# Loading each streamed slice of the query weights in two transfers, of 120 and of 8 rows

## Chip, core and metric

The kernel runs on one core of a Trainium2 chip. The metric is the device time of one launch in microseconds, as the median of several runs. Engines are named as in the profile: PE is TensorE's matmul stream and PEld its weight loads, DVE is VectorE, ACT is ScalarE, POOL is GpSimd, SP is SyncE, whose queue issues nearly all transfers from HBM.

## What is computed

Two layers are applied in turn, A, B, A, B, each to the layer norm of its input and added to it. The sequence has 2048 tokens of 640 values.

```python
# A: attention with a memory that is carried from segment to segment
mem = mem0                                   # 8 rows
for s in range(64):                          # segments of 32 tokens
    h = concat([mem, x[32*s : 32*s+32]])     # 40 rows
    q, k, v = h @ Wq, h @ Wk, h @ Wv         # 640 -> 32 heads x 192
    p = softmax(mask(q @ k.T * 192**-0.5))
    o = (p @ v) @ Wo                         # back to 640
    mem, out[s] = o[:8], o[8:]
# B: token mixing and a two-layer MLP
h   = gelu(layernorm(x) @ w1)
x1  = x + shifted_quarters(h) @ w2
out = x1 + gelu(layernorm(x1) @ w3) @ w4     # 640 -> 1536 -> 640
```

The memory makes A a recurrence: segment s+1 needs the output of segment s. All weights are bf16[...].

## The kernel before

The two A layers run as two lanes of one pipeline. Step t works on segment t of the first A layer and on segment t-5 of the second, so that each weight tile is used for 2 x 40 = 80 columns. There are 69 steps (`T_A = NSEG + LAG`). Between them `chunk` and `chunk_end` do layer B for 64 tokens of each lane, once in two steps.

In a step, `attention_step` goes through four pairs of head groups (`NPAIR`), each group of four heads. For a pair, `proj_pair` makes keys, queries and values, in this order. The weights of one pair and kind are a matrix of 640 x 1536, held as five slices of 128 rows (`KC = 5`, `PW = 1536`). Some slices stay on chip for the whole run; the others are streamed again in every step:

```python
STREAM = {"k": 3, "q": 3, "v": 2}
RING_A = 7
```

So a step streams four times three key, three query and two value slices, 8 x 4 = 32 transfers of 128 rows x 3072 bytes. `load_pair` adds one SP operation for each (line 431), into one of seven ring slots called `wst`. Each slice is used by 12 matmuls with their weight loads (line 507). `load_b` streams layer B's weights through three slots called `wstB` (lines 454 to 460). Resident slices (`wk`, `wq`, `wv`, and `wo`) are loaded once, at line 415.

The order of all work is made ahead of time: every operation is added to a `Plan` with an engine, an estimated duration and a due time, and `place` lays them out in time, each engine taking the earliest possible operation with the earliest due time. SP's operations have an estimated duration of `DMA_ISSUE` (0.37 us in the plan). The planned transfer service (`srv`) limits how early a transfer may be placed; one that is placed at that limit is called `paced`. When the program is written out in the planned order, each paced transfer is made to wait for the last PE operation planned to be done by then:

```python
        elif o.paced:
            k = len(done) - 1
            while k >= 0 and done[k].end + PE_LAT > o.start:
                k -= 1
            if k >= 0:
                tc.add_manual_dep(o.last, done[k].last.name, dep, reason="pace")
```

Apart from this, a transfer waits until its slot was read by PE, and until the transfer that used its landing semaphore before has landed. SP's transfers use eight such semaphores in turn. A matmul group's first weight load waits for the slice's semaphore.

## Time and profile before

| | |
|---|---|
| median of three runs | 3676.43 us (3671.96 to 3677.07) |
| the profiled execution's own time | 3664.71 us |
| its span, first to last instruction | 3663.0 us |
| mean granted TensorE clock | 0.982 |
| mean transfer rate over the span | 302 GB/s |
| issues of streamed query, key and value slices | 828, 828 and 552 |
| issues of layer B's weights | 525 of 320 KB and 140 of 160 KB |

The profile is of one execution. A row of the waits names the waiting engine and line, then what released it, the total in us, how often, and the longest. A row of the transfer queues gives packets, megabytes, and the time of the packets as a share of 16 transfer engines over the span. A row of issues shows SP's instruction, with the least, median and greatest time that SP spent on it. Apart from these views the prediction uses single records of the trace: the start and length of each transfer packet, and the times at which semaphores were raised.

### The profile page before, as it was taken

To read this page: it belongs to the slowest core of one execution; us is meant where nothing else is said; L and a number is where in the kernel's file an instruction comes from. 1 tells how busy PE (TensorE), PEld (TensorE's weight loads), DVE (VectorE), ACT (ScalarE), POOL (GpSimd) and SP (SyncE) were. 2 spreads that over 40 slices of the span, in tenths; PEclk is the share of its full clock that TensorE was granted. 3 is DMA by queue.
4 is the path that set the end of the run, shared out by engine and by line. 5 is a ranking of instruction groups with operands and counts; after the bars stand their busy time and mean duration, and the time that the engine had idled before them with its cause. 6 is when DMAs were issued, how large, how long until landed. Compare 5 with 4: busy or idle time off the path is not lost. (4 is left out here: it accounts for less than half of the span.)

```text
span 3663.0 us, 188705 instructions
## 1 busy us (share of the span) xinstructions
PE 3438.2 (94%) x84703; PEld 3279.3 (90%) x84703; DVE 2583.9 (71%) x7716; ACT 1530.9 (42%) x3586; POOL 247.8 (7%) x467
## 2 busy tenths in 40 slices
PE   5889999999999999999999999999999999999984
PEld 4788999999999999999999999999999999998873
DVE  2456777777777777777777777777777777776653
ACT  1233444444444444444444444444444444443331
POOL 0000000000000000000000000000000000000000
PEclk9999999999999999999999999999999999999996
DMA  9898988889888988889888898888988998889993
GB/s 318 296 313 293 319 301 304 303 311 322 307 301 302 313 311 304 304 306 322 305 309 306 299 322 302 309 306 300 322 295 309 309 313 309 297 296 304 317 304 111
DMA packets 512602, 1107.61 MB, mean 302 GB/s; under 512 B 50862, under 2 KB 223036, under 8 KB 511792
## 3 DMA queue, kind: packets, MB, share of 16 engines
q1 hardware_dynamic: 504560, 1082.42, 86.2%
q8 instruction: 662, 10.85, 1.2%
q0 software_dynamic: 7232, 13.13, 1.1%
q14 instruction: 148, 1.21, 0.1%
HBM read 1090.10 MB, written 5.24 MB: 299 GB/s over the span
## 5 line engine op out<-in xcount | busy, mean ns | idle before, releaser
L507 PEld LDWEIGHTS <-wst 128*128 128x128 bf16 x26496 | 1091.8, 100 | 108.3 <-DMA wst<-in_A_Wq_dram 42.8
L632 PE MATMUL psy<-oT,wo 128*128 128x80 bf16 (+1 forms) x16560 | 666.8, 199 | 35.6 <-issue 17.9
L632 PEld LDWEIGHTS <-wo 128*128 128x128 bf16 x16560 | 614.8, 100 | 42.8 <-issue 24.0
L517 ACT CAST qT<-psq 128x480 bf16<-128x480 f32 (+1 forms) x552 | 286.2, 529 | 791.8 <-PE psq L507 790.8
L507 PE MATMUL psq<-hT,wst 128*128 128x80 bf16 (+1 forms) x9936 | 494.5, 199 | 33.9 <-DMA wst<-in_A_Wq_dram 30.4
L507 PE MATMUL psk<-hT,wst 128*128 128x80 bf16 (+1 forms) x9936 | 477.5, 199 | 17.7 <-DMA wst<-in_A_Wk_dram 15.5
L621 DVE CAST oT<-pso 128x480 bf16<-128x480 f32 (+1 forms) x552 | 339.3, 619 | 193.7 <-PE pso L615 190.6
L507 PE MATMUL psv<-hT,wv 128*128 128x80 bf16 (+1 forms) x9936 | 432.9, 199 | 2.6 <-issue 2.6
L579 DVE CUSTOM_DVE_ANT_1 pss<-pss,mask 80x320 f32<-80x320 f32 (+1 forms) x512 | 244.9, 478 | 208.7 <-PE pss L568 165.4
L507 PEld LDWEIGHTS <-wv 128*128 128x128 bf16 x9936 | 383.5, 100 | 9.2 <-issue 3.1
L553 ACT COPY V<-pvt 80x384 bf16<-80x384 bf16 (+1 forms) x552 | 261.8, 474 | 270.0 <-PE pvt L544 249.6
L507 PE MATMUL psv<-hT,wst 128*128 128x80 bf16 (+1 forms) x6624 | 354.4, 199 | 13.7 <-DMA wst<-in_A_Wv_dram 6.8
L605 ACT COPY PT<-pst 80x320 bf16<-80x320 bf16 (+1 forms) x552 | 221.9, 402 | 320.6 <-PE pst L600 248.9
L531 DVE CAST kT<-psk 64x160 bf16<-64x160 f32 (+1 forms) x1104 | 336.6, 305 | 8.9
L537 ACT CAST vF<-psv 128x480 bf16<-128x480 f32 (+1 forms) x552 | 290.4, 526 | 122.4 <-PE psv L507 119.5
L507 PE MATMUL psk<-hT,wk 128*128 128x80 bf16 (+1 forms) x6624 | 319.0, 199 | 15.9 <-ACT hT L650 11.3
L507 PE MATMUL psq<-hT,wq 128*128 128x80 bf16 (+1 forms) x6624 | 318.9, 199 | 5.3 <-DMA wq<-in_A_Wq_dram 3.1
L525 DVE CAST kT<-psk 128x320 bf16<-128x320 f32 (+1 forms) x552 | 255.5, 463 | 96.9 <-PE psk L507 89.3
L586 ACT ACTIVATE Pm<-pss,sm 80x320 bf16<-80x320 f32 (+1 forms) x552 | 275.5, 504 | 101.4 <-DVE sm L579 100.8
L590 DVE TENSOR_REDUCE sm<-Pm 80x4 f32<-80x320 bf16 (+1 forms) x552 | 250.2, 453 | 75.9 <-ACT Pm L586 67.6
L544 PE MATMUL pvt<-ident,vF 128*80 128x128 bf16 (+1 forms) x3312 | 285.4, 223 | 8.2 <-ACT vF L537 5.3
L551 DVE COPY V<-pvt 80x384 bf16<-80x384 bf16 (+1 forms) x552 | 190.6, 349 | 139.0 <-ACT V L553 118.8
(108 smaller groups left out, 4561.5 us busy)
## 6 DMA issues: line engine op xcount, KB each, us to landing
wst<-in_A_Wk_dram SPq DMA_DIRECT2D x828, 384.0 KB, 5.0
wst<-in_A_Wq_dram SPq DMA_DIRECT2D x828, 384.0 KB, 5.0
wst<-in_A_Wv_dram SPq DMA_DIRECT2D x552, 384.0 KB, 5.0
wstB<-in_B_w_dram SPq DMA_DIRECT2D x525, 320.0 KB, 4.8
wstB<-in_B_w_dram SPq DMA_DIRECT2D x140, 160.0 KB, 4.6
wo<-in_A_Wo_dram SPq DMA_DIRECT2D x8, 960.0 KB, 7.4
wv<-in_A_Wv_dram SPq DMA_DIRECT2D x4, 1152.0 KB, 7.0
wk<-in_A_Wk_dram SPq DMA_DIRECT2D x4, 768.0 KB, 6.1
```

Of the source, the lines that this page charges most:

```text
L507: nc.tensor.matmul(out=o[:, cc, 0:N], lhsT=wv(kc, GW * j + cc * P, GW * j + (cc + 1) * P), rhs=h[:, kc, c0:c0 + N], start=(kc == 0 and cc ...
L517: nc.scalar.copy(out=q[:, :, 0:N], in_=T(pq)[:, :, 0:N])
L525: nc.vector.tensor_copy(out=k4[:, :, 0::3, 0:N], in_=p4[:, :, 0::2, 0:N])
L531: nc.vector.tensor_copy(out=k4[r0:r1, :, jj, 0:N], in_=p4[r0:r1, :, 1, 0:N])
L537: nc.scalar.copy(out=vf[:, :, 0:N], in_=T(pq)[:, :, 0:N])
L544: nc.tensor.transpose(out=o[0:N, c * P:(c + 1) * P], in_=vf[:, c, 0:N], identity=ident[:, :])
L553: nc.scalar.copy(out=dst, in_=src)
L579: nc.vector.tensor_tensor_reduce(out=o, in0=o, in1=maskt.unsqueeze(1).to_broadcast([N, HG, N]), scale=-scale, scalar=3.0e38, op0=ALU.add, ...
L586: nc.scalar.activation(out=Pb[0:N, :, 0:N], in_=o, func=ACT.Exp, bias=sm_[0:N, 0:1], scale=-1.0)
L590: nc.vector.tensor_reduce(out=sm_[0:N, 2:2 + HG], in_=Pb[0:N, :, 0:N], axis=AX.X, op=ALU.add)
L621: nc.vector.tensor_copy(out=o_[:, :, 0:N], in_=T(pso)[:, :, 0:N])
L632: nc.tensor.matmul(out=o[:, m, c0:c0 + N], lhsT=wo[:, cc, m * P:(m + 1) * P], rhs=o_[:, cc, 0:N], start=st, stop=True, skip_group_check=True)
```

## The change

Each streamed slice of the query weights is loaded by two transfers into the same slot: rows 0 to 119, then rows 120 to 127. Streamed key and value slices stay as they were, with one transfer. The plan counts two issues for such an operation, and the wait for pace goes to the first of its two transfers.

```diff
             def fn(op, b=b, kc=kc):
-                nc.sync.dma_start(out=T(b)[:, 0:PW], in_=w_src[kind][:, kc, cols])
-            add("SP", DMA_ISSUE, due - now + 0.01 * j, fn, w=(b,), dma=2 * P * PW, queue="wa")
+                if kind == "q":
+                    nc.sync.dma_start(out=T(b)[0:120, 0:PW], in_=w_src[kind][0:120, kc, cols])
+                    nc.sync.dma_start(out=T(b)[120:P, 0:PW], in_=w_src[kind][120:P, kc, cols])
+                else:
+                    nc.sync.dma_start(out=T(b)[:, 0:PW], in_=w_src[kind][:, kc, cols])
+            add("SP", DMA_ISSUE * (2 if kind == "q" else 1), due - now + 0.01 * j, fn, w=(b,), dma=2 * P * PW, queue="wa")
             slots.append(b)
...
         o.last = nc.cur_bb.bb.instructions[-1]
+        first = nc.cur_bb.bb.instructions[-2] if o.e == "SP" and o.d > DMA_ISSUE else o.last
...
-                tc.add_manual_dep(o.last, done[k].last.name, dep, reason="pace")
+                tc.add_manual_dep(first, done[k].last.name, dep, reason="pace")
```

## Prediction

> **What bounds the kernel now.** I read the page first, then the busy time by stretch, then the waits of TensorE, then SP's queue, and last the single records of transfers and semaphores.

> ```profile
> span 3663.0 us, 188705 instructions
> PE 3438.2 (94%) x84703; PEld 3279.3 (90%) x84703; DVE 2583.9 (71%) x7716; ACT 1530.9 (42%) x3586; POOL 247.8 (7%) x467
> ...
> q1 hardware_dynamic: 504560, 1082.42, 86.2%
> q8 instruction: 662, 10.85, 1.2%
> ```

> TensorE is busy 94% of the span, and the transfer engines spend 86.2% of it on SP's queue q1. VectorE and ScalarE have room. The stretch table says that the middle is fuller than the average:

> ```profile
> 500.00:1000.00 500.00, 489.76 (x12036) 473.34 (x12034) 376.33 (x1089) 224.34 (x511) 34.48 (x63) 1.00 0.90 309
> ```

> The columns after the length are PE, PEld, DVE, ACT, POOL, then the clock, the transfer engines' share and GB/s. PE is busy 489.8 of 500 us at full clock, transfers 0.90. So the bound is TensorE, with a weight stream close behind it, and a change of the stream can act only on the idle remainder. What that remainder waits for:

> ```profile
> PEld L507 <- DMA wst<-in_A_Wq_dram: 42.8, 80, 3.7
> PEld L507 <- issue: 35.5, 74, 1.7
> ...
> PEld L507 <- DMA wst<-in_A_Wk_dram: 23.7, 47, 2.4
> ...
> PEld L507 <- DMA wst<-in_A_Wv_dram: 11.4, 28, 0.7
> ```

> Columns: total us, times, longest. Streamed weights stop the weight loads for 42.8 + 23.7 + 11.4 = 78 us, the query weights most. "Issue" is a wait that nothing in the profile explains. PE has 60 gaps of over 0.25 us without a releaser, 46 us in all; I set them beside the packets of q8, the instruction stream, and 57 of them end 1.0 to 2.0 us after the end of such a 16 KB packet. There TensorE waits for its own instructions.

> The issue side:

> ```profile
> L431 SPq DMA_DIRECT2D wst<-in_A_Wq_dram x828: 327/328/1695, 9.9 to 3569.2; - x166
> ...
> DMA to landing us min/median/max: 3.2/5.0/7.4
> ```

> An issue takes SP 0.328 us (median), a load lands 5.0 us after it. The smallest step from issue to issue is 0.379 us; after a query load it is never below 0.706. SP is paced by PE (its largest wait is for psk), so it has time.

> **One engine ends the loads.** In the semaphore records a load posts 16 completions. Between first and last lie 1.83 us (median), and the last is 0.54 us behind the fifteenth. This last one is one and the same engine: its distance to the eighth is 1.12 us half a microsecond after the start of an instruction packet and 1.70 us two microseconds after it, while the fifteenth stays at 0.74 to 0.84. An instruction packet takes 1.04 us; 662 of them on one engine are 689 us, 18.8% of the span, on top of its 86.2%. These sums count overlapping packets, but this engine has no reserve. Which number it has, the trace does not say.

> [...]the load of h2u at the start posts one early update and then 8, where a 128-row load posts 16. No 120-row transfer is shown.[...]

> **The change, part by part.** The order of instructions on PE, VectorE, ScalarE and GpSimd stays as it was, and SP's order too, with each of the 828 query loads doubled.

> 1. *SP.* 828 more issues at 0.328 us are 272 us of SP time, one beside each query load; the eight-row load of h2u took 0.36 us, so I price both halves alike. A pair takes 0.379 + 0.328 = 0.71 us, and the next issue came after 0.706 us at the least: nothing is pushed. The pace's wait moves to the first half, so the second does not stand behind it. Were a 120-row issue to cost 0.6 us, some gaps would be overrun by up to 0.3 us; that is inside the ladder below. Upside: none.
> 2. *Landing semaphores.* SP's transfers take eight in turn, and an issue waits until the transfer eight places earlier has landed. Now that margin is 2.4 us or more in 99 of 100 cases. With pairs, eight places hold fewer loads: putting the old times into the new sequence, 133 of 3101 issues come too early, by 50 us together, 90 of them value loads. Queued behind a held value load are the next key loads and TensorE's first value group; their slack (next item) hides most of it. My count gives 1 to 3 us.
> 3. *Rows.* A 3072-byte packet takes 121 ns (median) and a semaphore packet 9. [...]+130 ns a load, +828 x 0.130 = 108 us each, 2.9% of the span. Three query loads come close together, so the delay adds up to 0.39 us where the engine has no pause; laid on the issue times, it is 0.19 us in the mean.[...]
> 4. *Ports.* [...]Completions of a load are spread over some 1.3 us without the last, so a random pair is 0.43 us apart; my estimate is 0.25 us a load, with bounds 0 and 0.94.
> 5. *TensorE's second wait.* The first weight load of each query tile waits for two semaphores, the second in an instruction of its own. TensorE's sequencer has 247 such now, 51 ns each, and the matmuls after them start 36 ns after the one before, as everywhere: hidden[...]. Where PE really waits (about 160 times) it may show: 0 to 8 us; I take 2.

> **What lateness costs.** For each query load I took the time from landing to first use. Of 828, 133 have under 0.1 us, 195 under 0.3, 259 under 0.5, 391 under 1.0. Making all of them late by d, summing what exceeds the slack, and crediting each stall to the loads already in flight gives:

> | d, us | 0.13 | 0.26 | 0.45 | 0.6 | 1.0 |
> |---|---|---|---|---|---|
> | added, us | 11 | 25 | 50 | 74 | 145 |

> **Forecast (0.53): slower.** The last completion of a query load is on a nine-row engine and later than the last one now, either because the slow engine is among them[...]. d = 0.19 + 0.25 = 0.44 us, about 49 us by the ladder; + 2 for held issues, + 2 for the second wait = 53. Against the profiled execution's own 3664.7 us this is 3718. That execution is 0.3% below the median of the runs, 3676.4; on their scale I give 3726, rounding the sum to 50. The case's own range is +11 (rows alone) to +145, so 3687 to 3821. Against it: the slow engine may be the one that is spared.

> **Rival 1 (0.33): faster, because engine 15 is the slow one.** Then query loads end on the next engine: -0.54 + 0.19 = -0.35 us, and key and value loads profit too. Of the waits for streamed weights, 0.36 us each would give back 24 (query) + 13 (key) + 9 (value) = 46 us; each stall removed takes slack from the loads in flight, so I count 60%, 28 us. Instructions come in sooner as well: a quarter of 46 us, 12. Together -40: 3636, between -10 and -80. It decides at a port loss of about 0.35 us a load: above that, nothing of it is left.[...]

> **Rival 2 (0.14): within 0.2%**, 3676. The slow engine is one of 8 to 14, or relief and ports cancel. A microsecond or two of held issues is all. For it: what is not last costs nothing.

> **Rival 3 (within the 0.53, 0.05 of it): the 120 rows are dealt differently[...]**, over eight engines. Then these take 15 + 1 rows, 0.97 us more a load, 803 us each, 22% on top of 86.2%: they exceed the span, and the end is at 1.08 x 3663, over 3950.

> **Numbers.** A difference of 0.2%, 7 us, is about what can be told from none. Faster 0.33, same 0.14, slower 0.53. The likeliest case gives 3726; the range goes from 3622, most of rival 1, to 3805, which leaves out the upper end of the port bound and rival 3: about 0.1 on each side.

> **What the profile after would show.** Rows: q1's packets up by some 828 x 7 = 5,800, with the same bytes. Forecast right: the waits for in_A_Wq grow from 42.8 to about 90 us, and those for key and value stay or grow. Rival 1: waits for Wq, Wk, Wv and "issue" all shrink. Item 1 wrong: the median issue of a query half is well above 0.33 us. Item 2 wrong: SP's waits name transfers for over 100 us, and value waits grow. The forecast falls if the waits for Wq do not grow; its mechanism falls if the end is later while Wq's waits stay.

## The result, and the profile after

The changed kernel takes 4079.7 us (median of four runs, 4076.0 to 4088.0) against 3674.7 us before (median of four): 1.111 times as long, 95% interval 1.109 to 1.113, or +405 us. I had forecast slower, with 3726 us and a range up to 3805. The direction was right and the size was wrong by a factor of eight.

The page of the changed kernel, the lines that answer to those of before:

```profile
span 4086.3 us, 190432 instructions
PE 3539.9 (87%) x84703; PEld 3343.0 (82%) x84703; DVE 2584.9 (63%) x7716; ACT 1533.1 (38%) x3586; POOL 248.0 (6%) x467
...
q1 hardware_dynamic: 510356, 1082.45, 88.5%
q0 software_dynamic: 7232, 13.13, 1.2%
q8 instruction: 666, 10.91, 1.2%
```

TensorE fell from 94% to 87%, while the transfer engines' share on q1 rose, from 86.2% to 88.5%, of a span that is 423 us longer. The bytes are the same. So SP's packets took 0.885 x 4086 = 3616 us of each engine's time where they had taken 0.862 x 3663 = 3157: 459 us more, somewhat more than the 405 us lost. 5,796 packets came in, 828 x 7 as foreseen, and those are far too few to explain it: the packets themselves became slower. The mean 3072-byte packet in the records went from 140 to 162 ns, and 31% of them lie between 160 and 260 ns, where before 92% had taken less than 130.

The loss is not all waiting. Of the 423 us, 102 are busy time of PE, for the same 84,703 matmuls. The mean granted clock fell from 0.982 to 0.966; by an estimate, 3438 x (0.982 / 0.966 - 1), that accounts for 57 of them. The other 321 us are idle time. Kernels of this case that lost more show a lower clock, by and large (0.981 at +121 us, 0.976 at +302, 0.967 at +391); that the stalls lowered it is not shown.

The stretch from 500 to 1000 us (PE, PEld, DVE, ACT, POOL, clock, transfers' share, GB/s):

```profile
500.00:1000.00 500.00, 443.32 (x10514) 424.46 (x10512) 328.03 (x951) 196.06 (x445) 32.06 (x58) 0.98 0.90 269
```

The same 0.90 of busy transfer engines now moves 269 GB/s, not 309.

The waits of the weight loads:

```profile
PEld L511 <- DMA wst<-in_A_Wq_dram: 293.0, 313, 2.3
PEld L511 <- issue: 73.1, 136, 2.4
PEld L511 <- DMA wst<-in_A_Wk_dram: 63.0, 92, 2.4
```

All waits for streamed weights went from 78 to 359 us, +281, of which +250 at query slices and +39 at key slices, with -9 at value slices. The waits called "issue" at this line doubled. SP's own issues stayed cheap:

```profile
L432 SPq DMA_DIRECT2D wst<-in_A_Wq_dram x828: 324/325/1683, 9.9 to 3991.9; - x166
L433 SPq DMA_DIRECT2D wst<-in_A_Wq_dram x828: 271/297/1647, 10.3 to 3992.4; - x166
```

The profile has no time to landing for this kernel, because the eight-row half posts other numbers of completions. Read from the semaphore records, the 120-row half lands 6.35 us after its issue (median; 5.02 before for 128 rows), the eight-row half 5.49, and the value slices that follow 5.96 instead of 4.94. The key slices land as soon after their issue as before (5.0 us), although their waits grew: these loads were issued late for TensorE.

### The profile page after: what moved, and what is told of

Read it like the earlier page. It is cut to its first block, busy times and chain, and to the rows that moved or that the text cites. A ratio compares the mean times of both kernels' runs of the same rounds, so it can differ in the third digit from the quotient of the medians.

```text
span 4086.3 us, 190432 instructions
## 1 busy us (share of the span) xinstructions
PE 3539.9 (87%) x84703; PEld 3343.0 (82%) x84703; DVE 2584.9 (63%) x7716; ACT 1533.1 (38%) x3586; POOL 248.0 (6%) x467
## 3 DMA queue, kind: packets, MB, share of 16 engines
q1 hardware_dynamic: 510356, 1082.45, 88.5%
## 5 line engine op out<-in xcount | busy, mean ns | idle before, releaser
L511 PEld LDWEIGHTS <-wst 128*128 128x128 bf16 x26496 | 1114.1, 100 | 417.8 <-DMA wst<-in_A_Wq_dram 293.0
L511 PE MATMUL psq<-hT,wst 128*128 128x80 bf16 (+1 forms) x9936 | 532.1, 201 | 277.5 <-DMA wst<-in_A_Wq_dram 268.4
L636 PE MATMUL psy<-oT,wo 128*128 128x80 bf16 (+1 forms) x16560 | 676.5, 200 | 64.3 <-issue 41.2
L511 PEld LDWEIGHTS <-wq 128*128 128x128 bf16 x6624 | 271.8, 100 | 22.9 <-DMA wq<-in_A_Wq_dram 9.3
```

What stands on the lines that cost most here:

```text
L511: nc.tensor.matmul(out=o[:, cc, 0:N], lhsT=wv(kc, GW * j + cc * P, GW * j + (cc + 1) * P), rhs=h[:, kc, c0:c0 + N], start=(kc == 0 and cc ...
L636: nc.tensor.matmul(out=o[:, m, c0:c0 + N], lhsT=wo[:, cc, m * P:(m + 1) * P], rhs=o_[:, cc, 0:N], start=st, stop=True, skip_group_check=True)
```

## Experiments

The theory after seeing this, under the name **ports** in the expectations: which partitions a transfer writes sets how long its packets take, and with 120 rows each packet slows down. The runs ask whether that is so; what in the hardware would do it they do not show. Rivals: the **ninth row** on eight engines; the **issue** side (twice the issues, places in the ring of eight landing semaphores, a second wait). A second question was how packet time becomes kernel time: through the **lateness** of single loads, as in my ladder, or as **throughput** of a stream without reserve.

### The transfers by themselves

```python
for i in range(64):
    nc.sync.dma_start(out=wt[i % 8][0:120, :], in_=W[0:120, kc(i), cols(i)])   # and the other kinds
```

> Not the layers: SP alone loads rows of 3072 bytes back to back, 64 loads of each kind, TensorE idle; the output is a copy of x. Kinds: 128, 120, 112, 96 rows, 64 rows at partitions 0 to 63, 64 rows at 32 to 95, pairs of 120 and 8, pairs of 128 rows in two column halves, 8 rows. All theories: 128 rows about 0.95 to 1.1 us a load[...]. Port theory: 120 rows up to 1.9 us though the bytes are fewer, a pair of 120 and 8 about 2 us or more, 112 and 96 rows slower than their bytes (0.83 and 0.71), 64 rows at 0 to 63 about 0.94 us and at 32 to 95 about 0.47. Ninth-row theory: 120 rows 0.95, a pair 1.07. Issue theory (two issues, two semaphores): 120 rows 0.95, and both kinds of pairs equally slow.

SP's issues in this run, one line for each kind in the order of the list, with the first and last start of 64 loads:

```profile
L54 SPq DMA_DIRECT2D wt<-in_A_Wq_dram x64: 327/328/624, 44.8 to 103.3; - x64
L56 SPq DMA_DIRECT2D wt<-in_A_Wq_dram x64: 324/325/410, 104.3 to 190.4; - x64
...
L62 SPq DMA_DIRECT2D wt<-in_A_Wq_dram x64: 465/465/553, 337.1 to 401.2; - x64
L64 SPq DMA_DIRECT2D wt<-in_A_Wq_dram x64: 509/591/602, 402.2 to 444.3; - x64
L66 SPq DMA_DIRECT2D wt<-in_A_Wq_dram x64: 324/325/593, 445.0 to 544.9; - x64
...
L69 SPq DMA_DIRECT2D wt<-in_A_Wq_dram x64: 327/328/431, 546.5 to 614.2; - x64
```

The stretches inside these phases, for 128 rows, 120 rows, 64 rows from partition 0 and 64 rows from partition 32 (the last two columns are share and GB/s):

```profile
58.00:103.00 45.00, 0.00 (x0) 0.00 (x0) 1.00 1.03 402
118.00:190.00 72.00, 0.00 (x0) 0.00 (x0) 1.00 0.97 263
...
350.00:401.00 51.00, 0.00 (x0) 0.00 (x0) 1.00 1.03 201
416.00:444.00 28.00, 0.00 (x0) 0.00 (x0) 1.00 0.93 306
```

From the thirteenth load of each kind on, the step between issues was

| kind | us a load | packet, ns (median) |
|---|---|---|
| 128 rows | 0.98 | 125 |
| 120 rows | 1.40 | 180 |
| 112 rows | 1.22 | 176 |
| 96 rows | 1.00 | 172 |
| 64 rows, partitions 0 to 63 | 0.99 | 251 |
| 64 rows, partitions 32 to 95 | 0.64 | 121 |
| pair of 120 and 8 rows | 1.57 | 178 |
| pair of 128 rows x 768 columns | 1.05 | 67 (half the size) |
| 8 rows | 0.45 | 214 |

Of the three theories only the port theory fits, if not in every size: it had the pair at 2 us or more (1.57 measured) and 64 rows at 32 to 95 at 0.47 (0.64; there SP's own issue, 0.591 us in the median, sets the step).

The 64 rows are the clean case: same bytes, and only the partitions differ, with the rows read from HBM shifted by the same 32. At 0 to 63 the median packet takes twice as long as at 32 to 95 (251 against 121 ns), 64 rows cost as much as 128 (0.99 and 0.98 us) and the rate is 201 GB/s; at 32 to 95 the median packet is as fast as with 128 rows (125 ns).

120 rows lie between: they cost 0.42 us a load more than 128, under the upper bound of 0.94 in item 4. What makes this size is open. It is not a mixture of fast and slow packets: of 6,037 packets in this stretch all took 158 to 212 ns. Reading from HBM was not varied apart from the partitions, so for 120 and 112 rows the partitions written are the likeliest cause of the loss, not a proven one, and what in the hardware slows these packets is not shown. The eight rows add 0.17 us on top, column halves 0.07. A split query load thus takes +0.59 us of stream time; 828 of them are 489 us, and the profile shows 459.

### Two transfers without uneven rows

```diff
-  dma_start(out=T(b)[0:120, 0:PW], in_=w_src[kind][0:120, kc, cols])
-  dma_start(out=T(b)[120:P, 0:PW], in_=w_src[kind][120:P, kc, cols])
+  c0 = cols.start
+  dma_start(out=T(b)[:, 0:768], in_=w_src[kind][:, kc, c0:c0 + 768])
+  dma_start(out=T(b)[:, 768:PW], in_=w_src[kind][:, kc, c0 + 768:c0 + PW])
```

> The changed kernel with each query slice split by columns instead of rows: two transfers of 128 rows x 768 columns. It keeps the doubled issues, the two semaphores and the wait's place, and takes away the uneven rows and the shifted blocks. Port theory: within 1% of before, 3665 to 3710 us. Ninth-row theory: the same. Issue theory (places in the ring of eight semaphores, SP's time, the second wait): most of the loss stays, 3950 to 4080 us.

Measured: 1.003 times before (1.002 to 1.004), 3677.3 us, and the waits for streamed weights add up to 88 us, against 78 before:

```profile
span 3675.9 us, 189604 instructions
...
q1 hardware_dynamic: 623792, 1082.48, 87.0%
...
PEld L512 <- DMA wst<-in_A_Wk_dram: 31.2, 55, 1.8
PEld L512 <- DMA wst<-in_A_Wq_dram: 28.6, 64, 1.8
PEld L512 <- DMA wst<-in_A_Wv_dram: 28.1, 36, 2.4
```

So twice the issues, twice the semaphores and the second wait cost some 10 us together, with 0.870 x 3676 - 3157 = 41 us more packet time. The issue theory falls as the cause of the loss.

### Even rows in shifted blocks

```diff
-  dma_start(out=T(b)[0:120, 0:PW], in_=w_src[kind][0:120, kc, cols])
-  dma_start(out=T(b)[120:P, 0:PW], in_=w_src[kind][120:P, kc, cols])
+  dma_start(out=T(b)[0:112, 0:PW], in_=w_src[kind][0:112, kc, cols])
+  dma_start(out=T(b)[112:P, 0:PW], in_=w_src[kind][112:P, kc, cols])
```

> The changed kernel with rows split 112 and 16: both over all 16 engines, 7 + 1 rows on each, so the rows are even again[...]. Port theory: still clearly slower than before, 3850 to 4100 us. Ninth-row theory: back to before, 3670 to 3700. Issue theory: as after, about 4080.

Measured: 1.082 times before (1.078 to 1.085), 3968.6 us, +302.

```profile
PEld L511 <- DMA wst<-in_A_Wq_dram: 224.5, 258, 2.5
```

Every query transfer posts 16 completions here (59,561 in all). I read that as seven rows and one on every engine, eight again, and three quarters of the loss are still there. The ninth row is not the main cause.

### 120 rows alone

```diff
-  dma_start(out=T(b)[120:P, 0:PW], in_=w_src[kind][120:P, kc, cols])
...
-  return T(slots[kc - nres])[:, c0:c1]
+  return T(slots[kc - nres])[0:(120 if kind == "q" else P), c0:c1]
...
-  rhs=h[:, kc, c0:c0 + N], start=(kc == 0 and cc == 0),
+  rhs=h[0:(120 if kind == "q" and kc >= nres else P), kc, c0:c0 + N], start=(kc == 0 and cc == 0),
```

> The changed kernel without its second transfer: rows 120 to 127 of the streamed query slices are neither loaded nor multiplied (the matmuls on them use 120 rows). One issue and one semaphore a load, no ninth row, fewer bytes than before. Port theory: a 120-row load took 1.40 us in the bulk run against 0.98 for 128 rows, +0.42 of the pair's +0.59, so 0.42/0.59 x 407 = +290 us: 3900 to 4000. Ninth-row theory: 3640 to 3680.

Measured: 1.087 times before (1.083 to 1.091), 3986.1 us, +314.

```profile
PEld L510 <- DMA wst<-in_A_Wq_dram: 260.1, 321, 2.2
```

One transfer a load, fewer bytes, and most of the loss. What is left for the eight rows is 405 - 314 = 91 us. SP's waits for earlier transfers to land are 16 us here, as before the change, against 390 us in the changed kernel; so these waits come with the loss and do not make the main part of it. Whether they have a part in the 91 us I did not separate.

### Halves

```diff
-  dma_start(out=T(b)[0:120, 0:PW], in_=w_src[kind][0:120, kc, cols])
-  dma_start(out=T(b)[120:P, 0:PW], in_=w_src[kind][120:P, kc, cols])
+  dma_start(out=T(b)[0:64, 0:PW], in_=w_src[kind][0:64, kc, cols])
+  dma_start(out=T(b)[64:P, 0:PW], in_=w_src[kind][64:P, kc, cols])
```

> The changed kernel with rows split 64 and 64, four rows an engine in each, even over all engines. 64 rows at partitions 0 to 63 took 0.99 us in the bulk run, as long as 128 rows. Port theory, if the two halves follow each other in step on all engines: +0.99 us a load, 0.99/0.59 x 407 = +680: about 4350; if engines drift apart so that some write the lower half while others write the upper,[...] it can come down to some 3750. Ninth-row theory and issue theory: 3675 to 3700, as with column halves.

Measured: 1.108 times before (1.105 to 1.112), 4063.4 us. It is between the two ends: 391 us for 828 loads is 0.47 us each, half of what halves in step would cost. That the engines drift apart, as the expectation had it, is one reading of this and is not shown. It is as bad as 120 and 8, with 16 completions for each half: q1 has 517,808 packets, 828 x 16 more than before. But it is a less clean run than the two before it:

```profile
L432 SPq DMA_DIRECT2D wst<-in_A_Wq_dram x828: 465/546/1781, 10.0 to 3954.6; - x166
L433 SPq DMA_DIRECT2D wst<-in_A_Wq_dram x828: 465/588/1851, 10.6 to 3955.1; - x166
...
PEld L511 <- DMA wst<-in_A_Wq_dram: 190.7, 177, 2.0
PEld L511 <- issue: 180.1, 267, 2.6
```

SP's issues take longer for 64 rows, and some 40% of the weight loads' new waits are "issue" waits, without a releaser in the profile. What the longer issues cost was not measured.

### How the loss grows with the number of split loads

```diff
-  if kind == "q":
+  if kind == "q" and kc == KC - STREAM["q"]:      # one of three
...
-  if kind == "q":
+  if kind == "v":                                  # value slices instead
```

> The changed kernel with only the first of the three streamed query slices of a pair split 120 and 8 (276 of 828 loads). If the weight stream as a whole has become the bound (throughput theory) and there was no reserve before, a third of the loss: 3674 + 136 = 3810. If a reserve has to be used up first, 3690 to 3740. If only the lateness of query loads against their slack counts (my ladder, 0.59 us on a third of the loads), about +25: 3700.

> The changed kernel with the value slices split 120 and 8 instead of the query slices (552 loads instead of 828). Throughput theory: what counts is the number of split loads, 552/828 x 407 = +271: about 3945, and the waits that grow are not those for value slices alone. Lateness theory: value slices had the least waiting before (11.4 us against 42.8), so less than half of that, 3700 to 3800, and the waits for Wv take all of it.

Measured: one of three 1.034 times before (1.031 to 1.038), 3794.0 us; value slices 1.065 (1.062 to 1.068), 3905.3 us. Span and queue of the one-third run, then of the value run:

```profile
span 3789.7 us, 189300 instructions
...
q1 hardware_dynamic: 506492, 1082.43, 87.9%
...
span 3909.9 us, 189880 instructions
...
q1 hardware_dynamic: 508424, 1082.44, 89.0%
```

In a row:

| split loads | packet time by the bulk prices | added packet time an engine (share x span) | added time |
|---|---|---|---|
| 276 query | +163 | +174 | +121 |
| 552 value | +326 | +322 | +233 |
| 828 query | +489 | +459 | +405 |

Each split load costs 0.42 to 0.49 us from the first third on. A reserve, if there is one, is small: the column halves' 41 us of packet time cost a quarter of their size, the 174 us of a third already 70%. The ladder's +25 for a third falls. In the run with split value slices the waits show that the loss is not confined to the late loads:

```profile
PEld L511 <- DMA wst<-in_A_Wv_dram: 119.2, 178, 1.9
PEld L511 <- DMA wst<-in_A_Wq_dram: 106.1, 136, 3.9
PEld L511 <- issue: 55.2, 111, 2.7
```

Query loads were left alone there, and their waits grew from 43 to 106 us. Value loads had waited 11 us before and now cost as much apiece as query loads in the one-third run. By the semaphore records the loads issued next after a split one land late too: the unsplit query slices of the one-third run 5.9 us after their issue, the key slices of the value run 5.8, where both took 5.0 before. The query slices of the value run landed only 0.2 us later, so landing times do not account for all of their waits.

### A lighter stream

```diff
-  dma_start(out=T(b)[:, 0:PW], in_=w_src[kind][:, kc, cols])
+  if kind == "q":
+      dma_start(out=T(b)[:, 0:GW], in_=w_src[kind][:, kc, cols.start:cols.start + GW])
...
+  if kind == "q":
+      return T(slots[kc - nres])[:, c0 % GW:c0 % GW + c1 - c0]
```

> The kernel before with half of each streamed query slice: 128 rows x 768 columns in one transfer, no shifted blocks; both head groups of a pair multiply with the same half, so the second group's streamed query weights are left out, and 0.16 GB are not loaded; TensorE's instructions stay the same in number. Asks whether the weight stream already set the pace before the change. Throughput theory: 828 x 0.45 us less packet time; if the stream alone set the pace, 0.7 to 0.9 of it comes back, -260 to -330 us, 3350 to 3410. If TensorE set it too (both at their limit), only its waits can go, and its busy 3438 us stay: -60 to -130 us, 3545 to 3615. If neither, as before.

Measured: 0.974 times before (0.972 to 0.976), 3577.4 us, -91. From its page:

```profile
span 3579.3 us, 188705 instructions
...
PE 3412.9 (95%) x84703; PEld 3270.9 (91%) x84703; DVE 2582.6 (72%) x7716; ACT 1530.8 (43%) x3586; POOL 246.4 (7%) x467
...
q1 hardware_dynamic: 504560, 919.63, 79.2%
```

The packets' time fell by 3157 - 0.792 x 3579 = 322 us, and 91 came back, with TensorE then at 95%. So before the change the kernel stood near a corner: lighter transfers give a quarter of their time back, and heavier ones, from 170 us of packet time on, cost 70 to 90% of it. What makes the corner was not taken apart. The engines' share in the middle stretch is 0.90 before and after, and a load that lands later also holds one of the seven ring slots longer; no run changed the ring.

### Which engine carries TensorE's instructions

```python
for i in range(23000):                   # 16000 in the first run
    nc.tensor.matmul(out=ps[:], lhsT=lw[:], rhs=rw[:], start=True, stop=True)
...
for i in range(224):                     # here 7 rows; also 2, 4, 6 and 8. The first run is without the step of 18
    nc.sync.dma_start(out=wt[i % 8][0:109:18, :], in_=W[0:7, kc(i), cols(i)])
```

Engine numbers, here and in the prediction, are names by row count: engine 7 is the one that the eighth row brings in, engine 15 the one of the sixteenth. That more rows add engines to those that fewer rows use is an assumption. The traces show the count alone: the second run has 13,504 packets under 512 bytes, which are 512 for the copies of x and 224 x 58 = 12,992 for its loads of 2 to 16 rows, one completion a row. So the row count from which loads are late beside an instruction packet tells how early in that order its engine comes.

> Not the layers: TensorE runs 16000 small matmuls, and beside it SP loads 6, 7, 8, 14, 15 and 16 rows of 3072 bytes, 224 loads of each; the output is a copy of x. Asks which transfer engine also carries TensorE's instructions. An instruction packet takes about 1.04 us, so a load that shares its engine with one has a last completion about 0.5 to 1 us behind the others.[...] The theory that the spared engine does not matter (ports did the damage) takes no side here; the forecast's first branch (slow engine among 0 to 7) needs it at 8 rows or fewer.

> Not the layers: as the run with few rows, with TensorE's matmuls going on throughout, but 2, 4, 6, 7 and 8 rows go to every 18th partition[...]; then 15 and 16 rows at partitions from 0 on; the output is a copy of x. The earlier run showed late last completions with 14 and 15 rows and left 6 to 8 open. A late last completion soon after an instruction packet must appear from the row count on that includes the engine[...]. The forecast's first branch needs it at 8 rows or fewer, rival 1 (engine 15) only at 16.

## Why the prediction was wrong

**Direction right, size wrong: two steps failed.**

*Item 4, ports, was under-sized.* It was an estimate: 0.25 us a load, from how far apart completions lie, for a delay that no trace had shown. The transfers by themselves show 0.42 for the 120 rows. With the eight rows' 0.17 (item 3 had 0.13 for the row) a load takes +0.59 us instead of my 0.38. My upper bound of 0.94 held the 0.42. This alone moves the ladder to +72. The forecast also put the last completion on an engine with nine rows. Most of the loss comes without a ninth row (120 rows alone, +314 us), so a slow engine among those with nine is not its main reason.

*The ladder, "what lateness costs", was the step that failed.* It asked of each load how late it is against its own slack, and credited every stall to the loads in flight. Here each load also took the engines' time, and the loads issued next landed late as well: query slices 1.3 us later, not 0.44, value slices 1.0 us later though nothing of theirs was changed. Even that does not reach the loss on the ladder: 1.3 us for the query slices gives +205, with 1.0 us for the value slices about +245, both estimates from the trace of before. The warning was in my own numbers: a 0.90 share in the middle stretch, instruction blocks included, and "a weight stream close behind". I let the stream act on the late load alone. The runs with a third, with value slices and with 120 rows alone put in its place a rule of this kernel: added packet time (174 and 322 us, and 0.884 x 3973 - 3157 = 355) x 0.7 to 0.9. It is read off, not derived; which part goes through the engines, which through SP's later issues and which through the lower clock stays open.

*"This last one is one and the same engine"* was wrong. The rhythm after an instruction block was real (1.12 and 1.70 us), and by the second run I had read a sequence of different engines, each late after its own block, as one. Nor are all 662 blocks on one engine: spread over eight in turn their 689 us are, by an estimate, some 2.4% of the span each, not 18.8%. Rival 1 rested on it. It falls: with 15 rows every block already made a load late, so by elimination none is left for the sixteenth engine, and a load that spares it gains nothing by that. That it was the slow one no trace had shown.

*Item 1* was right in the price: 0.325 and 0.297 us for the halves. That the next issue never came sooner than 0.706 us after a query load was misread: it did in 25 of 828 cases, at the least after 0.38 us, some 8 us at most (column halves cost 10 us in all). *Item 2*: I counted 50 us of held issues with the old landing times; with loads landing later SP waits 390 us for transfers. Of my own test of that item the first half came true (over 100 us), so it was wrong in size; the second did not, the value waits fell from 11.4 to 2.6 us. The main loss comes without these waits (120 rows alone). *Item 3* was right in the count of rows: on the eight semaphores that SP's loads use in turn there are 53,765 updates, just what 16 for a 128-row or 120-row transfer and 9 for an eight-row one add up to, and of the 16 of a 120-row transfer one comes at once, 5.8 us before the last. I read these counts as 120 rows over 15 engines and 8 over 8, and rival 3 falls with that. *Item 5* was small as foreseen: the column halves have the same second waits and lose 10 us in all.

*Rival 2* needed 120 rows that cost no more than the spared engine gives back, and falls with the bulk run (1.40 against 0.98 us).

## What to carry to other kernels

Before splitting or reshaping a transfer, ask which partitions it will write: from partition 0, 64 to 120 rows took as long as 128 or longer here (64 rows 0.99 us, 112 rows 1.22, 120 rows 1.40, against 0.98). Splitting by columns kept all 128 and cost 0.3%. Price a transfer by itself, back to back, and multiply: in this kernel, with the transfer engines busy 0.9 of the time, 70 to 90% of a large addition became kernel time, whatever the slack of the single load. A slack count that asks only the delayed loads misses those behind them.

## What the runs showed of the hardware

- 64 rows of 3072 bytes at partitions 0 to 63 take 0.99 us a load, at partitions 32 to 95 0.64 us (SP's issue sets that step); packets 251 against 121 ns in the median. 120 rows from partition 0 take 1.40 us a load, 128 rows 0.98; I had expected +0.25 us, and it is +0.42.
- Beside TensorE's instruction blocks of 16 KB the last completion of a load came up to 1.85 us late, in the runs with small matmuls: with 6 rows at every eighth block, with 7 and 8 rows at two of eight, with 14 at all but one of eight, with 15 at every block; with 2 and 4 rows at none. I read this as eight engines in turn.
- With slower weight packets TensorE's instructions come more slowly too: an instruction packet took 1.04 us in the mean before and 1.13 after, and all "issue" waits of the weight loads grew from 108 to 178 us.
